# A Fourier mixing layer with a feed-forward layer behind it: input of the second in units of four columns s, other block sizes at both ends, and stages placed anew

## The chip, the core and the metric

The kernel runs on one NeuronCore of a Trainium2 chip. Its engines work side by side, each through its own list of instructions in order: TensorE (PE in the profile; PEld are its weight loads), VectorE (DVE), ScalarE (ACT), GpSimd (POOL) and SyncE (SP), of which the last two issue most transfers (DMAs) here. An instruction that has to wait for another engine holds up everything behind it in its own list. The metric is device time in microseconds (us), taken from the runs without the profiler; one more execution was recorded by the profiler, and all durations below come from it.

## The reference

```python
X = np.fft.rfft(x, axis=1)                  # x: 8 batches x 3008 tokens x 256 features
Y = X * (filt_r + 1j * filt_i)[None]
x = np.fft.irfft(Y, n=3008, axis=1).reshape(8 * 3008, 256)
h = x @ w_in                                # 256 x 2048
g = np.maximum(h, 0.0) + alpha * np.minimum(h, 0.0)
out = g @ w_out                             # 2048 x 256
```

The inputs and the output are float32. The kernel computes with float16 operands and float32 sums.

## The kernel before

**The two layers.** The Fourier layer is done as matmuls, with 3008 = 47 x 64: a token is 64 * s1 + s, with s1 from 0 to 46 and s from 0 to 63. Its result for two batches at a time lies in the SBUF tile yT, with the features on the partitions and 2 x 3008 columns, one for each token. The feed-forward layer reads columns of yT in blocks. A block of 512 columns (class Block) has 16 steps. Step j does `up(j)`: two matmuls that give 128 of the 2048 hidden features, into one half of a PSUM tile hps of two halves (two such tiles exist). After each second step ACT copies the pair from hps to SBUF as gtb (L420), and DVE applies the slope alpha in three instructions (two at L423, one at L424). In the same steps the block before does its `down(j)` (L433): in all, for each 128 columns, 16 matmuls that sum over the hidden features into a PSUM tile op, which ACT copies out as osb (L438); SP stores it to the output (L396). A block needs the last gtb of a pair of ups only in a late part of the next block's first steps: with n groups of 128 columns, step q of the next block does the downs n*q to n*q+n-1, and each 128 columns need all 16 hidden tiles.

There are four pairs of batches. `sizes` is the same for each: five blocks of 512 columns, one of 384, six of 512, so 12 blocks and 192 steps a pair, 768 steps in all.

**The Fourier stages.** They are cut into pieces that are put between the steps by hand: `put(step, ...)` notes a piece for a step, and it is issued just ahead of that step's ups. Each piece takes one of two PSUM banks (psF), which it holds until ACT or DVE has copied the result out; which of the two is decided when the program is built. The pieces of a batch are:
- a, 16 of them (L164): the first transform, copied by ACT (asb); after each four of them `save_a` writes to DRAM, and `turn_a` reads all back turned (at).
- b, 12 (L184): the second transform; DVE reads the result twice, for the products ww and uu (L188, L189). POOL moves ww across the partitions (sw), and from batch 2 on DVE adds both (`piece_s`).
- c, 12 (L209): the first inverse transform, copied by ACT (v); `turn_c` writes v to DRAM and, after the last, reads it back as zt.
- d, 16 (L231): the last transform, copied into yT by ACT.

`plan_fft(b, a0, ga, ta, b0, gap, add, lag, d0, ...)` gives a batch its steps: the a pieces from a0 every ga steps, `turn_a` at ta, the b pieces from b0 every gap steps, c lag steps behind b, d from d0. Batch 0 (class First) has no DRAM in between: its c pieces are followed by t pieces (L310, transposes on PE, copied to zt) and d pieces. Four t and four d of it stand ahead of the first block, the other twelve of each are put into the first 47 steps. `neg` (L476) makes the negated filter for batches 1 and on in steps 27 to 33.

**The order inside yT.** The columns of a batch are not in the order of tokens. Before, they lie in four groups of 752 columns (16 values of s), each with two halves of 376 for the two halves of s (0 to 31, 32 to 63), as wi3 gives both halves at once; inside, 47 values of s1 by eight values of s. A d piece gives four of the eight values of s for 128 of the 256 features, so its copy writes runs of four columns, and four d pieces fill 752 columns. The order that matters around the change is:

```python
g, dh, mh = i // 4, (i // 2) % 2, i % 2
t0 = self.base + g * 752
```

and a store of 128 columns (`store`) is cut where a run of 376 columns ends, since each run goes to its own rows of the output, eight rows in a run.

Of the kernel before, what the change touches and what calls it, by code (L numbers as in the profile page):

```python
# [13 lines left out]
NFFT = 3008  # L14
N1 = 47
N2 = 64
NK1 = 24
D = 256
NB = 8
DFF = 2048  # L20
NH = 32
# [43 lines left out]
def kernel(  # L65
# [53 lines left out]
    yT = konst.tile([128, 2, 2 * NFFT], FP16, name="yT")  # L119
# [5 lines left out]
    def load_x(b, c):  # L125
        xs = p_x.tile([2 * N1, 8 * D], FP16, name="xs")
        for h in range(2):
            nc.gpsimd.dma_start(out=xs[h * N1 : h * N1 + N1], in_=xrow(b, h, c))  # L128
        return xs
# [12 lines left out]
    def bank(wide=False):  # L142
        if wide:
            return psH.tile([128, 2, 512], FP32, name="hps")[:, 0]
        return psF.tile([128, 512], FP32, name="psF")


    class Fft:
# [75 lines left out]
                    nc.sync.dma_start(out=self.zt[:, s], in_=v_dram[self.b, :, s])  # L224

        def piece_d(self, i, evict, wide=False):
            g, dh, mh = i // 4, (i // 2) % 2, i % 2
            pd = bank(wide)
            ps = pd[:, 0 : 8 * N1].rearrange("p (m x) -> p m x", m=4)
            for m in range(4):  # L230
                nc.tensor.matmul(ps[:, m], self.zt[:, 8 * g + 4 * mh + m, dh * 128 : dh * 128 + 128],  # L231
                                 wi3_s, start=True, stop=True)
            t0 = self.base + g * 752
            evict(yT[:, dh, t0 : t0 + 752].rearrange("p (x m) -> p x m", m=8)[:, :, 4 * mh : 4 * mh + 4],
                  ps.rearrange("p m x -> p x m"))

    def on_act(o, i):
        nc.scalar.activation(o, i, AF.Copy)  # L238
# [4 lines left out]
    both = (on_act, on_dve)  # L243
# [72 lines left out]
    f0 = First()  # L316
# [24 lines left out]
    def warm(n):  # L341
        pw = psO.tile([128, 2, D], FP32, name="op")
        for _ in range(n):
            nc.tensor.matmul(pw[:, 0, 0:128], id16, id16, start=True, stop=True)
# [25 lines left out]
            f0.piece_b(kp + 2)  # L370
    nc.gpsimd.dma_start(out=filts_s[0:64], in_=filt_s[64:128])
    warm(8)
    for i in range(4):
        f0.piece_t(i, both[i % 2], i % 2 == 1)
    warm(4)
    for i in (0, 2, 1, 3):
        f0.piece_d(i, both[i // 2], i > 1)


    sizes = [512] * 5 + [384] + [512] * 6  # L380
    blocks = []
    for p in range(NB // 2):
        t = 0
        for n, tn in enumerate(sizes):
            blocks.append((p, t, tn, 2 * p + (n >= 6)))
            t += tn

    def store(p, t0, osb, lane):
        t = t0
        while t < t0 + 128:  # L390
            b, r = 2 * p + t // NFFT, t % NFFT
            blk, o = r // 376, r % 376
            n = min(t0 + 128 - t, 376 - o)
            g, h = blk // 2, blk % 2
            row = b * NFFT + (o // 8) * N2 + NH * h + 8 * g
            nc.sync.dma_start(  # L396
                out=bass.AP(tensor=out.tensor, offset=out.offset + row * D,
                            ap=[[N2 * D, n // 8], [D, 8], [1, D]]),
                in_=osb[t - t0 : t - t0 + n, lane])
            t += n  # L400

# [2 lines left out]
    class Block:  # L404
# [22 lines left out]
        def down(self, q):  # L427
            n = self.tn // 128
            for w in range(n * q, n * (q + 1)):
                si, k = w // 16, w % 16  # L430
                if si % 2 == 0 and k == 0:
                    self.op = psO.tile([128, 2, D], FP32, name="op")
                nc.tensor.matmul(self.op[:, si % 2], self.gts[k][:, 128 * si : 128 * si + 128],  # L433
                                 wout_s[:, k], start=(k == 0), stop=(k == 15))
                if k == 15 and (si % 2 == 1 or si == n - 1):
                    m = si % 2 + 1
                    osb = p_osb.tile([128, 2, D], FP32, name="osb")
                    nc.scalar.activation(osb[:, 0:m], self.op[:, 0:m], AF.Copy)  # L438
                    for lane in range(m):
                        store(self.p, self.t0 + 128 * (si - m + 1 + lane), osb, lane)  # L440
# [3 lines left out]
    def put(step, fn, *args):  # L444
        plan.setdefault(step, []).append((fn, args))

    def plan_fft(b, a0, ga, ta, b0, gap, add, lag, d0, quarters, x_at):
        f = Fft(b)
        for i in range(16):
            put(int(a0 + ga * i), f.piece_a, i, on_act)  # L450
        for c in range(4):
            put(int(a0 + ga * (4 * c + 3)), f.save_a, c)
            if b + 1 < NB:
                put(x_at[c],
                    lambda b=b, c=c: xc.update({(b + 1, c): load_x(b + 1, c)}))
        for q in range(quarters):
            w = NK1 // quarters
            put(ta, f.turn_a, nc.sync, w * q, w * q + w)
        bs = [b0 + (2 * int(gap * kp / 2) if add else int(gap * kp)) for kp in range(12)]
        for kp in range(12):  # L460
            put(bs[kp], f.piece_b, kp)
            if add:
                put(bs[kp] + add, f.piece_s, kp)
            put(bs[kp] + lag, f.piece_c, kp, on_act)
        for q in range(4):
            put(bs[3 * q + 2] + lag + 1, f.turn_c, q)
        for i in range(16):
            put(d0 + min(i, 4) + 2 * max(i - 4, 0), f.piece_d, i, on_act)

    for g, t0, d0, gap, evs in ((1, 0, 6, 1, both), (2, 17, 25, 2, (on_dve,)), (3, 32, 40, 2, (on_act,))):  # L470
        for i in range(4):
            put(t0 + gap * i, f0.piece_t, 4 * g + i, evs[i % len(evs)])
            put(d0 + gap * i, f0.piece_d, 4 * g + i, evs[i % len(evs)])

    def neg(ka, kb):
        nc.vector.tensor_scalar(filts_s[64:128, ka:kb], filt_s[64:128, ka:kb], -1.0, None, OP.mult)  # L476
# [1 line left out]
        nc.gpsimd.dma_start(out=filt_s[64:128, ka:kb], in_=filt_s[0:64, ka:kb])  # L478

    for i in range(4):  # L480
        put(27 + 2 * i, neg, 6 * i, 6 * i + 6)
    plan_fft(1, 16, 1, 32, 40, 2.75, 0, 7, 92, 4, (20, 24, 72, 73))
    plan_fft(2, 66, 2, 97, 109, 4.5, 8, 13, 187, 4, (110, 114, 118, 122))
    for b in range(3, NB):
        p = 96 * (b - 1)
        plan_fft(b, p - 68 - 2 * (b > 3), 2.4 + 0.1 * (b > 3), p - 27, p + 5, 5, 8, 13, p + 91, 1, (p + 6, p + 10, p + 16, p + 20))

    prev = None
    step = 0
    for p, t0, tn, _ in blocks:  # L490
        blk = Block(p, t0, tn)
        for j in range(16):
            for fn, args in plan.pop(step, ()):
                fn(*args)
            blk.up(j)
            if prev is not None:
                prev.down(j)
            step += 1
        prev = blk
# [33 lines left out]
```

## Time and profile before

| | |
|---|---|
| three runs without the profiler | 797.7, 797.81, 800.44 us |
| median | 797.81 us |
| the profiled execution | 799.4 us |
| its span, first to last instruction | 797.5 us |
| first matmul of the first block (L414) | 39.37 us |
| first down (L433) | 50.57 us |
| start of block 6 (step 96), after 2944 columns | 141.07 us |
| one block of 16 steps without pieces (steps 704 to 751) | 13.89 us |
| a block with a, b and c pieces (steps 208 to 255) | 16.67 to 17.05 us |
| L420, ACT, 128x1024 / 128x768 | 1022 / 809 ns, 352 / 32 times |
| L423, DVE, 128x512 / 128x384 | 354 / 316 ns, 704 / 64 times |
| L424, DVE, 128x1024 / 128x768 | 692 / 558 ns, 352 / 32 times |
| L438, ACT, 128x512 / 128x256 | 594 / 379 ns, 92 / 4 times |
| L188 and L189, DVE, each | 683 / 679 ns, 84 times each |
| L238, ACT, copies of a / c / d | 594 / 595 / 484 ns |
| L241, DVE, copies of t / d | 681 / 542 ns |
| SP's waits for ACT ahead of stores (L396) | 152.6 + 110.3 + 56.2 + 42.4 us |

The span is the time from the first to the last instruction of the profiled execution. What was timed without the profiler has a median 0.3 us above that span. A duration in the profile of a PE, DVE or ACT instruction can overlap with the next one's start on the same engine, so that the distance from start to start, in the timeline, is what one costs where the engine is full. PE matmuls, for one: those of 512 columns have a mean duration of 379 ns and start 0.216 us apart.

### The profile page before, as it was taken

What the parts mean: (1) busy time and instruction counts of PE and PEld (TensorE: products, weight loads), DVE (VectorE), ACT (ScalarE), POOL (GpSimd) and SP (SyncE); (2) the same over time, 40 slices, a digit from 0 to 9 for tenths busy, and PEclk for the clock granted to TensorE, in tenths of its full rate; (3) what the DMA queues carried; (4) which work ended last, traced back from release to release, by engine and by line L of the source; (5) the groups of instructions that cost most, each with busy time, mean ns of one, the idle gap of its engine ahead of it and who ended that gap; (6) DMA issues with size and microseconds to landing.
All of it is one profiled execution on the core that took longest, in us unless ns stands there. A gap on an engine that the chain in (4) does not pass through costs nothing.

```text
span 797.5 us, 16176 instructions
## 1 busy us (share of the span) xinstructions
PE 778.6 (98%) x5980; PEld 542.8 (68%) x5980; DVE 645.7 (81%) x1449; ACT 597.6 (75%) x836; POOL 141.5 (18%) x272
## 2 busy tenths in 40 slices
PE   6999999999999999999999999999999999999997
PEld 6756667666667666766667666766666766776665
DVE  4787996798879987798877988799877999777773
ACT  3678678877778887788768877788877867686663
POOL 7511330132103210132102321032100221000000
PEclk9999999999999999999999999999999999999999
DMA  9967448574655447474483545754484243511111
GB/s 179 211 143 181 132 106 223 157 169 115 150 153 121 110 125 173 126 142 129 119 207 83 119 127 141 177 112 113 123 179 117 54 106 85 138 38 28 41 40 53
DMA packets 94360, 100.59 MB, mean 126 GB/s; under 512 B 11369, under 2 KB 82041, under 8 KB 94217
## 3 DMA queue, kind: packets, MB, share of 16 engines
q1 hardware_dynamic: 79512, 68.80, 32.8%
q0 software_dynamic: 14768, 30.75, 19.7%
q8 instruction: 47, 0.77, 0.4%
q14 instruction: 33, 0.26, 0.1%
HBM read 56.26 MB, written 46.66 MB: 129 GB/s over the span
## 4 chain that ended last, share of the span: by engine, by line
PE 90%; ACT 3%; DMA 2%; DVE 1%; issue 1%; SPq 1%; POOL 0%; ACTq 0%; DVEq 0%; POOLq 0%
PE op L433 39%; PE hps L414 39%; PE psF L164 3%; PE psF L231 3%; PE psF L209 2%; PE psF L184 2%; ACT gtb L420 2%; DMA xs<-in_x_dram 1%; DMA filt_s<-in_filt_i_dram 1%; ACT osb L438 1%; PE hps L281 1%; DMA a_dram<-asb 1%; ACT v L238 1%; SPq L396 1%; PE psF L310 1%
## 5 line engine op out<-in xcount | busy, mean ns | idle before, releaser
L420 ACT ACTIVATE gtb<-hps 128x1024 f16<-128x1024 f32 (+1 forms) x384 | 385.4, 1004 | 126.5 <-PE hps L414 126.1
L433 PE MATMUL op<-wout_s,gtb 128*128 128x256 f16 x3008 | 451.1, 272 | 0.6 <-DVE gtb L424 0.6
L414 PE MATMUL hps<-yT,win_s 128*128 128x512 f16 (+1 forms) x1536 | 449.1, 374 | 0.4 <-ACT gtb L420 0.2
L433 PEld LDWEIGHTS <-gtb 128*128 128x128 f16 x3008 | 293.2, 97 | 189.6 <-DVE gtb L424 0.9
L423 DVE TENSOR_SCALAR m<-gtb,alm_s 128x512 f16<-128x512 f16 (+1 forms) x768 | 237.9, 351 | 99.5 <-ACT gtb L420 97.3
L424 DVE TENSOR_TENSOR gtb<-gtb,m 128x1024 f16<-128x1024 f16 (+1 forms) x384 | 261.5, 681 | 24.8 <-PE hps L414 0.9
L191 POOL DMA_DIRECT2D sw<-ww x168 | 87.8, 527 | 483.8 <-DVE ww L188 480.9
L414 PEld LDWEIGHTS <-win_s 128*128 128x128 f16 x1536 | 144.9, 98 | 32.3 <-issue 4.3
L238 ACT ACTIVATE asb<-psF 96x512 f16<-96x512 f32 x112 | 66.5, 594 | 16.4 <-PE psF L164 16.3
L238 ACT ACTIVATE yT<-psF 128x376 f16<-128x376 f32 x120 | 58.1, 484 | 22.9 <-PE psF L231 22.5
L438 ACT ACTIVATE osb<-op 128x512 f32<-128x512 f32 x96 | 56.2, 585 | 6.1 <-issue 3.2
L188 DVE TENSOR_TENSOR ww<-psF,filts_s 128x512 f16<-128x512 f32 x84 | 57.4, 683 | 0.0
L189 DVE TENSOR_TENSOR uu<-psF,filt_s 128x512 f16<-128x512 f32 x84 | 57.1, 679 | 0.0
L238 ACT ACTIVATE v<-psF 128x512 f16<-128x512 f32 x84 | 50.0, 595 | 4.3 <-PE psF L209 4.3
L164 PE MATMUL psF<-xs,wf_s 94*96 94x512 f16 x112 | 42.6, 381 | 2.5 <-ACT v L238 2.1
L231 PE MATMUL psF<-wi_s,zt 96*128 96x94 f16 x504 | 41.9, 204 | 0.9 <-ACT yT L238 0.7
L128 POOL DMA_DIRECT2D xs<-in_x_dram x64 | 34.0, 542 | 29.6 <-PE psF L164 14.8
L231 PEld LDWEIGHTS <-zt 96*128 96x128 f16 x512 | 35.5, 97 | 5.1 <-issue 1.5
L184 PE MATMUL psF<-at,twf_s 128*128 128x256 f16 x168 | 32.0, 272 | 2.7 <-ACT v L238 1.7
L209 PE MATMUL psF<-uu,twi_s 128*128 128x256 f16 x168 | 33.4, 273 | 0.0
L196 DVE TENSOR_TENSOR uu<-uu,sw 128x512 f16<-128x512 f16 x72 | 30.1, 418 | 0.0
L209 PEld LDWEIGHTS <-twi_s 128*128 128x128 f16 x192 | 18.6, 98 | 2.8 <-DVE uu L189 0.4
(57 smaller groups left out, 200.0 us busy)
## 6 DMA issues: line engine op xcount, KB each, us to landing
out_dram<-osb SPq DMA_DIRECT2D x128, 128.0 KB
xs<-in_x_dram POOLq DMA_DIRECT2D x64, 188.0 KB, 4.4
a_dram<-asb SPq DMA_DIRECT2D x28, 384.0 KB
sw<-ww POOLq DMA_DIRECT2D x168, 64.0 KB, 2.1
v_dram<-v SPq DMA_DIRECT2D x112, 96.0 KB
zt<-v_dram SPq DMA_DIRECT2D x28, 384.0 KB
at<-a_dram SPq DMA_DIRECT2D x20, 384.0 KB
at<-a_dram SPq DMA_DIRECT2D x32, 96.0 KB
```

Of the source, the lines that this page charges most:

```text
L164: nc.tensor.matmul(ps[0:96], wf1_s, xs[:, o : o + 512], start=True, stop=True)
L188: nc.vector.tensor_mul(ww, px, filts_s[:, 2 * kp : 2 * kp + 2])
L191: nc.gpsimd.dma_start(out=sw[o : o + 64], in_=ww[64 - o : 128 - o])
L209: nc.tensor.matmul(pv[:, kh], twi_s[:, k1], u[:, kh], start=u is us[0], stop=u is us[-1])
L231: nc.tensor.matmul(ps[:, m], self.zt[:, 8 * g + 4 * mh + m, dh * 128 : dh * 128 + 128], wi3_s, start=True, stop=True)
L238: nc.scalar.activation(o, i, AF.Copy)
L414: nc.tensor.matmul(self.hps[:, j % 2, 0:tn], win_s[:, kt, j * 128 : (j + 1) * 128], yT[:, kt, self.t0 : self.t0 + tn], start=(kt == 0), st ...
L420: nc.scalar.activation(g[:, :, 0:tn], self.hps[:, :, 0:tn], AF.Copy)
L423: nc.vector.tensor_scalar(m[:, i, 0:tn], g[:, i, 0:tn], 0.0, a, OP.min, OP.mult)
L424: nc.vector.tensor_add(g[:, :, 0:tn], g[:, :, 0:tn], m[:, :, 0:tn])
L433: nc.tensor.matmul(self.op[:, si % 2], self.gts[k][:, 128 * si : 128 * si + 128], wout_s[:, k], start=(k == 0), stop=(k == 15))
L438: nc.scalar.activation(osb[:, 0:m], self.op[:, 0:m], AF.Copy)
```

## The change

The columns of yT now lie in units of four s: 16 runs of 188 columns to a batch (47 values of s1 by four of s), two of them (376 columns, one for each half of s) for each two d pieces. The numbering of d pieces changes with it: pieces 0 and 1 are now the two halves of the features for the same four s, and together they fill the first 376 columns; a piece's copy writes its 376 columns without a gap. A store is cut at each 188 columns, with four rows in a run: 312 stores in the built kernel, 248 before.

In the first pair the blocks have 256, 384, four times 512, 256 and six times 512 columns, so 13 blocks; in the last, 384 and 128 stand in place of the last 512. There are 800 steps, and the first pair has 16 more, so everything of batch 2 and later moves by 16 steps.

Ahead of the first block there are now two t and two d pieces. The other fourteen of each lie in steps 0 to 47 (t) and 4 to 68 (d), and DVE copies the t pieces but one and eleven of the d pieces. Batch 1 has its a at 20 to 38, `turn_a` at 40, b from 46 every 3.25 steps, d from 107 (before: 16 to 31, 32, 40 and 2.75, 92). Batch 2 has its a from 64 every 2.5 steps, `turn_a` at 103, b from 121 every 5, d from 203 (before: 66 and 2, 97, 109 and 4.5, 187). From batch 3 on the a pieces come in fours at 0, 5, 7 and 8 of ten steps in place of every 2.4 or 2.5. `neg` begins at 31, not 27.

```diff
         def piece_d(self, i, evict, wide=False):
-            g, dh, mh = i // 4, (i // 2) % 2, i % 2
+            g, mh, dh = i // 4, (i // 2) % 2, i % 2
...
-            t0 = self.base + g * 752
-            evict(yT[:, dh, t0 : t0 + 752].rearrange("p (x m) -> p x m", m=8)[:, :, 4 * mh : 4 * mh + 4],
-                  ps.rearrange("p m x -> p x m"))
+            t0 = self.base + 376 * (i // 2)
+            evict(yT[:, dh, t0 : t0 + 376].rearrange("p (x m) -> p x m", m=4), ps.rearrange("p m x -> p x m"))
...
     warm(8)
-    for i in range(4):
-        f0.piece_t(i, both[i % 2], i % 2 == 1)
+    for i in range(2):
+        f0.piece_t(i, both[i], i == 1)
     warm(4)
-    for i in (0, 2, 1, 3):
-        f0.piece_d(i, both[i // 2], i > 1)
-
-
-    sizes = [512] * 5 + [384] + [512] * 6
+    for i in range(2):
+        f0.piece_d(i, both[i], i == 1)
+
+
+    sizes = [[512] * 5 + [384] + [512] * 6 for _ in range(NB // 2)]
+    sizes[0] = [256, 384] + [512] * 4 + [256] + [512] * 6
+    sizes[-1] = [512] * 5 + [384] + [512] * 5 + [384, 128]
...
-            blk, o = r // 376, r % 376
-            n = min(t0 + 128 - t, 376 - o)
-            g, h = blk // 2, blk % 2
-            row = b * NFFT + (o // 8) * N2 + NH * h + 8 * g
+            half, o = r // 188, r % 188
+            n = min(t0 + 128 - t, 188 - o)
+            row = b * NFFT + (o // 4) * N2 + NH * (half % 2) + 4 * (half // 2)
...
-                            ap=[[N2 * D, n // 8], [D, 8], [1, D]]),
+                            ap=[[N2 * D, n // 4], [D, 4], [1, D]]),
...
-    def plan_fft(b, a0, ga, ta, b0, gap, add, lag, d0, quarters, x_at):
+    def plan_fft(b, sa, ta, b0, gap, add, lag, d0, quarters, x_at):
...
-            put(int(a0 + ga * i), f.piece_a, i, on_act)
+            put(sa[i], f.piece_a, i, on_act)
...
-            put(int(a0 + ga * (4 * c + 3)), f.save_a, c)
+            put(sa[4 * c + 3], f.save_a, c)
...
-    for g, t0, d0, gap, evs in ((1, 0, 6, 1, both), (2, 17, 25, 2, (on_dve,)), (3, 32, 40, 2, (on_act,))):
-        for i in range(4):
-            put(t0 + gap * i, f0.piece_t, 4 * g + i, evs[i % len(evs)])
-            put(d0 + gap * i, f0.piece_d, 4 * g + i, evs[i % len(evs)])
+    for i, t in zip(range(2, 16), (0, 1, 15, 17, 19, 21, 33, 35, 37, 39, 41, 43, 45, 47)):
+        put(t, f0.piece_t, i, on_act if i == 2 else on_dve)
+    for i, t in zip(range(2, 16), (4, 5, 20, 23, 26, 27, 39, 41, 52, 54, 58, 60, 66, 68)):
+        put(t, f0.piece_d, i, on_act if i in (2, 4, 6) else on_dve)
...
-        put(27 + 2 * i, neg, 6 * i, 6 * i + 6)
-    plan_fft(1, 16, 1, 32, 40, 2.75, 0, 7, 92, 4, (20, 24, 72, 73))
-    plan_fft(2, 66, 2, 97, 109, 4.5, 8, 13, 187, 4, (110, 114, 118, 122))
+        put(31 + 2 * i, neg, 6 * i, 6 * i + 6)
+    plan_fft(1, [int(20 + 1.25 * i) for i in range(16)], 40, 46, 3.25, 0, 7, 107, 4, (26, 31, 73, 80))
+    plan_fft(2, [int(64 + 2.5 * i) for i in range(16)], 103, 121, 5, 8, 13, 203, 4, (122, 126, 132, 136))
     for b in range(3, NB):
-        p = 96 * (b - 1)
-        plan_fft(b, p - 68 - 2 * (b > 3), 2.4 + 0.1 * (b > 3), p - 27, p + 5, 5, 8, 13, p + 91, 1, (p + 6, p + 10, p + 16, p + 20))
+        p = 96 * (b - 1) + 16
+        sa = [(121 if b == 3 else p - 91) + 21 + 10 * (i // 4) + (0, 5, 7, 8)[i % 4] for i in range(16)]
+        plan_fft(b, sa, sa[15] + 5, p + 5, 5, 8, 13, p + 91, 1, (p + 6, p + 10, p + 16, p + 20))
```

Step numbers below count from the first block. A letter with a number, as d10, is the piece and its place in its batch, from 0.

More of the change, by code (lines that the diff above doesn't have):

```diff
@@ L383 @@
         t = 0
-        for n, tn in enumerate(sizes):
-            blocks.append((p, t, tn, 2 * p + (n >= 6)))
+        for tn in sizes[p]:
+            blocks.append((p, t, tn))
             t += tn
@@ L480 @@
     for i in range(4):
-        put(27 + 2 * i, neg, 6 * i, 6 * i + 6)
-    plan_fft(1, 16, 1, 32, 40, 2.75, 0, 7, 92, 4, (20, 24, 72, 73))
-    plan_fft(2, 66, 2, 97, 109, 4.5, 8, 13, 187, 4, (110, 114, 118, 122))
+        put(31 + 2 * i, neg, 6 * i, 6 * i + 6)
+    plan_fft(1, [int(20 + 1.25 * i) for i in range(16)], 40, 46, 3.25, 0, 7, 107, 4, (26, 31, 73, 80))
+    plan_fft(2, [int(64 + 2.5 * i) for i in range(16)], 103, 121, 5, 8, 13, 203, 4, (122, 126, 132, 136))
     for b in range(3, NB):
-        p = 96 * (b - 1)
-        plan_fft(b, p - 68 - 2 * (b > 3), 2.4 + 0.1 * (b > 3), p - 27, p + 5, 5, 8, 13, p + 91, 1, (p + 6, p + 10, p + 16, p + 20))
+        p = 96 * (b - 1) + 16
+        sa = [(121 if b == 3 else p - 91) + 21 + 10 * (i // 4) + (0, 5, 7, 8)[i % 4] for i in range(16)]
+        plan_fft(b, sa, sa[15] + 5, p + 5, 5, 8, 13, p + 91, 1, (p + 6, p + 10, p + 16, p + 20))
     prev = None
     step = 0
-    for p, t0, tn, _ in blocks:
+    for p, t0, tn in blocks:
         blk = Block(p, t0, tn)
```

## The prediction

> **What bounds the kernel now.** First the page: its busy shares (part 1) and the shares of the chain that ended last (part 4).
>
> ```profile
> PE 778.6 (98%) x5980; PEld 542.8 (68%) x5980; DVE 645.7 (81%) x1449; ACT 597.6 (75%) x836; POOL 141.5 (18%) x272
> ...
> PE 90%; ACT 3%; DMA 2%; DVE 1%; issue 1%; SPq 1%; POOL 0%; ACTq 0%; DVEq 0%; POOLq 0%
> ```
>
> TensorE sets the end, and the change removes no matmul of it. So I looked for the time in which PE did not issue. From the timeline's matmul starts: 512 columns take 0.216 us from start to start, 256 take 0.109, 94 take 0.041, a transposing matmul of L310 0.089. So a piece costs PE: a 0.22, t 4 x 0.089 = 0.36, d 4 x 0.041 = 0.165, b 0.22, c 0.22 (0.43 in batch 1, which has four). With these, all work from the first block's first up matmul (39.37) to the end is 740.9 us, so it could end at 780.3. It ends at 792.5: 12.2 us are lost. The starts of L414 put them by block of 16 steps: 5.6 in blocks 0 to 5 (39 to 141 us), 2.2 in blocks 8 and 9, 3.4 in the later batches, 0.8 at the end, 0.2 elsewhere.
>
> The timeline shows the kind of loss, at step 66:
>
> ```profile
> 106.83 0.38 PE L184 MATMUL psF<-at,twf_s 128*128 128x256 f16 x2
> ...
> 108.55 1.02 ACT L420 ACTIVATE gtb<-hps 128x1024 f16<-128x1024 f32 x1 [0.38 <-PE hps L414]
> ...
> 109.01 0.68 DVE L188 TENSOR_TENSOR ww<-psF,filts_s 128x512 f16<-128x512 f32 x1
> 109.11 0.27 PE L209 MATMUL psF<-sw,twi_s 128*128 128x256 f16 x1
> ...
> 109.47 0.59 ACT L238 ACTIVATE v<-psF 128x512 f16<-128x512 f32 x1
> 109.61 0.68 DVE L189 TENSOR_TENSOR uu<-psF,filt_s 128x512 f16<-128x512 f32 x1
> ...
> 110.11 0.38 PE L164 MATMUL psF<-xs,wf_s 94*96 94x512 f16 x1 [0.73 <-ACT v L238]
> ```
>
> The c piece ends at 109.4, ACT copies v out until 110.06, and the a piece of the same step, which has the same one of the two psF banks, stands until 110.11: 0.89 us more than back to back. The second thing to see: the b piece issued at 106.83 is read by DVE from 109.01 to 110.29. DVE is 3.4 us behind PE, and a bank filled for DVE is held that long.
>
> DVE's pace in the first block, where it is saturated:
>
> ```profile
> 48.42 0.61 DVE L423 TENSOR_SCALAR m<-gtb,alm_s 128x512 f16<-128x512 f16 x2
> ...
> 49.06 0.69 DVE L424 TENSOR_TENSOR gtb<-gtb,m 128x1024 f16<-128x1024 f16 x1
> ...
> 49.67 0.61 DVE L423 TENSOR_SCALAR m<-gtb,alm_s 128x512 f16<-128x512 f16 x2
> ```
>
> One pair of ups costs DVE 1.25 us here, not the 1.40 that durations add up to. The end:
>
> ```profile
> 786.87 5.63 PE L433 MATMUL op<-wout_s,gtb 128*128 128x256 f16 x50 [0.59 <-DVE gtb L424]
> 789.09 0.60 ACT L438 ACTIVATE osb<-op 128x512 f32<-128x512 f32 x1 [3.23 <-issue]
> 792.58 0.60 ACT L438 ACTIVATE osb<-op 128x512 f32<-128x512 f32 x1 [2.90 <-PE op L433]
> ```
>
> **The change, part by part**, against the span of 797.5.
>
> *Start.* The first up now needs two t and two d pieces, not four and four. t1 is copied by DVE by 37.8, d0 and d1 by 38.9, so it starts at about 38.9, not 39.37: -0.5. The other two of each, 2 x (0.36 + 0.165) = 1.05, now lie in the loop: net +0.6.
>
> *Ramp, blocks 0 to 6 (2944 columns, as blocks 0 to 5 before).* No row has a 256-column pair. By the step from 512 to 384 (L423 starts 0.269 and 0.235 apart, L424 0.61 and 0.475) it is 0.84 on DVE; ACT's 128x512 rows give 0.595 (interval 0.48). Bounds: half of 1.25, and 1.04, the 384 pair. The two small blocks in place of one cost DVE 3.4 us more, and 10 copies move from ACT to DVE (6 t x 0.60 + 4 d x 0.46 = 5.4). Load in blocks 0 to 4: PE 70.7, DVE 73.0, ACT 51.7; before, PE 81.6, DVE 72.6. So DVE, which had 9 us of slack, has none. I walked each queue in order by these intervals, with the banks that the built kernel gives its pieces:
> - Block 0: ACT and its hand-over, 0.64 a pair, against PE 0.43; from 38.7 to 44.5 against 4.9 of work: lost 0.9. DVE is at 48.3 when it ends its last pair.
> - Block 1 (0.54 us a step): t at step 19 needs t4's bank, which DVE frees at 47.5: 1.1. d at 20 waits for t5's copy: 0.5, and the a behind it for ACT: 0.75. Then a pieces in the one ACT bank at consecutive steps, where the copy's round is 1.1 to 1.5: 1.75. Together 4.1.
> - Block 2: 0.4.
> - Block 3: c at 53 stands in the bank of d at 52, which DVE reaches late: 1.85; c at 56 behind d at 54: 0.55; b at 59 behind c of that step: 0.9; two more, 0.7. Together 4.0.
> - Block 4: steps 66, 69 and 79 have c and then a in one bank: 3 x 0.89 = 2.7. c at 66 behind b at 65: 1.05; c at 69 behind d at 68: 1.35; one more 0.2. Together 5.3.
>
> Behind each wait stand all later ups and downs on PE, so each counts in full: 14.7. But each wait lets DVE catch up, so such a list overstates: before, c at 69 two steps behind b in its bank cost nothing. I take 13. Lowest: the four same-bank follows by ACT (3.6), block 0 (0.7) and an ACT-bound block 1 (1.5): 5.8. Highest: DVE 3.4 behind at each wait on it: +3.1, 17.8. Against 5.6 before, the ramp costs +7.4 (+0.2 to +12.2).
>
> By the granted clock this region ran at 1.00, though the stretch 10 to 20 us, with single gaps of 1.2, had 0.92. [...]
>
> *Batch 2 and later.* The a pieces of batch 3 on go to places (0, 5, 7, 8 of ten) where no c or b is, and batch 2's b get the later batches' gap of 5. Before, a behind c cost 1.11 (step 140), 0.56 (145) and 0.51 (153), and then 0.51 once in each of four batches, ACT having copied osb, v and asb in a row:
>
> ```profile
> 285.96 0.59 ACT L438 ACTIVATE osb<-op 128x512 f32<-128x512 f32 x1
> ...
> 287.09 0.38 PE L184 MATMUL psF<-at,twf_s 128*128 128x256 f16 x2 [0.35 <-ACT v L238]
> ```
>
> Now c follows b in its bank by three steps, 3.3 us; here DVE ends 2.5 after b's issue (182.50 to 185.03). So nothing waits: 1.11 + 0.56 + 4 x 0.51 + 0.51 = -4.2. It could be -2 if ACT still copies three in a row.
>
> *End.* Behind the last up stand 3 + 14 downs of 0.109 (1.85 us) that don't need it; its ACT (0.38) and DVE copies (0.8 at 128 columns by the same step, 1.04 at most) take 1.4 or less: the wait of 0.76 goes. The last copy is 128x256, 0.38 not 0.60, and one store is issued behind it, not two of 0.62: -0.84. Together -1.6. 16 more steps of small matmuls cost PE nothing: columns and 0.057 us weight loads stay under 0.44 a step.
>
> *Queues.* 64 more stores on SP, 0.7 us each (three in 2.22 at 108.19): 45 us. SP waits for ACT over 450 us, which hides them. The last save of batch 1's a now goes at step 38 with no store between it and the at reads: copy 1.2, landing 2.7 (the chain's a_dram step), four issues of 0.44, landing 2.7: 8.4 against 8 steps of about 1 us to b at 46. 0.4 at most, taken into the ramp; with a store in between 0.7 more. On POOL the x loads move 6 to 8 steps, ahead of use by 11 or more; neg on DVE moves by 4 steps, used 8 or more later; batch 1's d start 18 steps behind turn_c, not 14. Nothing.
>
> **Sum:** 797.5 + 0.6 + 7.4 - 4.2 - 1.6 = 799.7. The profiled execution took 799.4 with a span of 797.5; the median of the runs is 797.81, so 0.3 over that span: 800.0.
>
> **Rivals.**
> - *A, the ramp loses no more than before* (5.6): 800.0 - 7.4 = 792.6. For it: block 0 is short, downs start at 44.5, not 50.57, and ACT has 5.4 us less. Against it: the four same-bank follows alone are 3.6. Chance 0.15.
> - *B, DVE's lag decides, and it is slower.* From block 1 on DVE never idles and runs 3.4 us behind as at step 64, so each c and t that follows a DVE piece waits its full lag: 17.8, so 804.8; it decides from a ramp loss of about 14.8, 801.8. For it: DVE's 73.0 against PE's 70.7. Against: the waits hand DVE idle time. Chance 0.31.
> - *C, the new places of a do not do what they should*: the 4.2 stays: 804.2. For it: osb, v and asb still share ACT. Against: no two pieces share a step. Chance 0.07.
> - Forecast: a ramp loss of 7 to 14.8, so 794 to 801.8: 0.47.
>
> **Numbers.** A measurement here tells 0.5%, 4.0 us: 793.8 and 801.8. Faster: 0.12 of A. Slower: B and C, 0.38. Same: the forecast and 0.03 of A, 0.50. Range 793.5 to 804.5, which leaves out about half of A and the ends of B and C; the forecast's own is 794 to 801.8.
>
> **What would show it.** First up near 38.9 and the first down near 44.5; a c start at step 53, and 66 and 69, more than 1 us behind its step; block 7's first up near 151 to 153; no a start over 0.3 us late from step 112 on; the last wait of PE on gtb gone and the last store landing some 4.2 us behind the last matmul. If the first up of block 7 comes before 146, my ramp is wrong and A holds.

## Result and profile after

The changed kernel takes 823.87 us (median of 6 runs, 821.84 to 824.25), the kernel before, run beside it, 798.69 (6 runs, 797.7 to 800.61): 1.0308 times as long, 95% interval 1.0289 to 1.0327. The forecast was 800.0, and the range ended at 804.5. The profiled execution's span is 821.6, 24.1 longer than that of before. Of all executions behind the times below, one, of e12, ran at a granted clock of 0.72 and took 1451.9 us; its ratio leaves that one out.

The page of the changed kernel, busy shares and chain:

```profile
PE 783.8 (95%) x6044; PEld 547.5 (67%) x6044; DVE 657.6 (80%) x1507; ACT 597.7 (73%) x843; POOL 141.2 (17%) x272
...
PE 79%; DMA 8%; DVE 4%; ACT 3%; SPq 2%; issue 1%; POOL 0%; ACTq 0%; POOLq 0%
```

PE's share of the chain went from 90% to 79%, and DMA's from 2% to 8%: about 50 us of the chain more than before lie in transfers. The waits view says which pieces stood for them (lost us, times, longest):

```profile
PEld L231 <- DMA zt<-v_dram: 11.1, 5, 3.7
...
PE psF L231 <- DMA zt<-v_dram: 9.7, 5, 3.5
...
PE psF L209 <- DVE yT L240: 3.1, 3, 1.4
```

L231 is the d piece. The first d of batches 2 to 6 (steps 203, 299, 395, 491, 587) stood 3.6, 2.1, 1.2, 3.1 and 0.6 for zt; before, none did. Only the last row is of the kind that the prediction was about, c behind a d piece that DVE holds.

Loss by block was measured as for the prediction: the length of a block less its matmuls at their distances from start to start.

| us | predicted | measured |
|---|---|---|
| first up, and 1.05 of t and d now in the loop | +0.6 | -0.7 (first up 37.66) |
| blocks 0 to 6 against 0 to 5 before | +7.4 (13.0 against 5.6) | +13.6 (19.2 against 5.6) |
| blocks after these | -4.2 | +10.7 (16.4 against 5.7) |
| end | -1.6 | about +0.3 |
| sum | +2.2 | +23.9 |

The first row needs care. Seven profiles, that of before among them, have the old first blocks and first stages. In four of them the clock stayed at 1.00 from 10 us up to the first block, and the first up came at 37.5 to 37.7. The other three show the clock at 0.50 for one or three times 3.41 us between 13 and 23.4 us (before: 18.4 to 21.9), and there it came at 39.1 to 40.5. The changed kernel's profile has no such stretch, so the 1.7 is mostly how the execution fell.

SP's own timeline around the end of a batch's FFT, where the save and the reads of at are batch 4's and v and zt are batch 3's (issues; start, time over the group, count):

```profile
322.08 0.38 SPq L169 DMA_DIRECT2D a_dram<-asb  x1
327.48 2.25 SPq L176 DMA_DIRECT2D at<-a_dram  x4
329.83 3.46 SPq L396 DMA_DIRECT2D out_dram<-osb  x3
333.33 1.93 SPq L218 DMA_DIRECT2D v_dram<-v  x4
338.65 1.73 SPq L224 DMA_DIRECT2D zt<-v_dram  x4
```

The same place in the kernel before:

```profile
302.71 0.32 SPq L169 DMA_DIRECT2D a_dram<-asb  x1
304.11 2.24 SPq L396 DMA_DIRECT2D out_dram<-osb  x3
306.46 2.31 SPq L176 DMA_DIRECT2D at<-a_dram  x4
311.23 1.55 SPq L396 DMA_DIRECT2D out_dram<-osb  x2
312.88 2.03 SPq L218 DMA_DIRECT2D v_dram<-v  x4
318.15 1.73 SPq L224 DMA_DIRECT2D zt<-v_dram  x4
```

In the changed kernel SP issues the save of a at 322.08 and then stands until 327.48, because the reads of at wait for the save to land: 5.4. Before, the same two stood 3.75 apart, and SP issued three stores in between. Behind them three stores take 3.46 to issue (before, two took 1.55), the v writes come at 333.33, and the reads of zt wait until 338.65 for these, 5.3 as before. The first d was due at about 340.4 and started at 342.47. The batch's whole last turn hangs on how fast single DMAs land, with stores ahead of them and beside them.

In the ramp the waits that the prediction's walk priced one by one are there. PE's timeline in blocks 2 (the first line) and 4:

```profile
77.55 0.38 PE L184 MATMUL psF<-at,twf_s 128*128 128x256 f16 x2 [1.28 <-DMA at<-a_dram]
...
103.91 0.28 PE L209 MATMUL psF<-uu,twi_s 128*128 128x256 f16 x1 [0.93 <-DVE uu L189]
...
105.20 0.38 PE L164 MATMUL psF<-xs,wf_s 94*96 94x512 f16 x1 [0.69 <-ACT v L237]
...
109.83 0.27 PE L209 MATMUL psF<-uu,twi_s 128*128 128x256 f16 x1 [1.25 <-DVE yT L240]
...
111.11 0.38 PE L164 MATMUL psF<-xs,wf_s 94*96 94x512 f16 x1 [0.68 <-ACT v L237]
...
111.76 1.01 PE L433 MATMUL op<-wout_s,gtb 128*128 128x256 f16 x4
112.57 1.06 PE L414 MATMUL hps<-yT,win_s 128*128 128x512 f16 x2
...
125.19 0.28 PE L209 MATMUL psF<-sw,twi_s 128*128 128x256 f16 x1 [1.04 <-DMA sw<-ww]
```

Against back to back these cost 1.09 and 0.85 at step 66 (walked: 1.05 and 0.89), and 1.42 and 0.85 at step 69 (1.35 and 0.89). Three things the walk did not have: the b of step 46 stands 1.45 for at (the first line; 0.4 at most was granted), a c at step 79 stands 1.21 for sw (the last), and from 111.8 on the matmuls take twice as long. The windows view (PE busy, PEld, DVE, ACT, POOL, then the granted clock, DMA share, GB/s):

```profile
108.40:111.80 3.40, 1.46 (x10) 0.74 (x9) 2.54 (x5) 0.88 (x2) 1.03 (x2) 1.00 0.03 7
111.80:115.20 3.40, 3.40 (x14) 1.81 (x13) 1.31 (x3) 1.49 (x3) 0.00 (x0) 0.50 0.56 147
```

3.4 us with little work, then 3.4 us at clock 0.50, which costs some 1.7. The same stands behind two of the zt waits, at 343.9 and at 535.0.

### The profile page after: what moved, and what is told of

It reads as the page before. It is cut to its first block, busy times and chain, and to the rows that moved or that the text cites. A ratio compares the mean times of both kernels' runs of the same rounds, so it can differ in the third digit from the quotient of the medians.

```text
span 821.6 us, 16481 instructions
## 1 busy us (share of the span) xinstructions
PE 783.8 (95%) x6044; PEld 547.5 (67%) x6044; DVE 657.6 (80%) x1507; ACT 597.7 (73%) x843; POOL 141.2 (17%) x272
## 4 chain that ended last, share of the span: by engine, by line
PE 79%; DMA 8%; DVE 4%; ACT 3%; SPq 2%; issue 1%; POOL 0%; ACTq 0%; POOLq 0%
PE op L433 34%; PE hps L414 33%; PE psF L164 3%; PE psF L231 3%; PE psF L209 2%; DMA v_dram<-v 2%; DMA zt<-v_dram 2%; PE psF L184 2%; DMA at<-a_dram 2%; ACT gtb L420 2%; DVE m L423 1%; SPq L396 1%; DVE gtb L424 1%; DMA xs<-in_x_dram 1%; DMA sw<-ww 1%
## 5 line engine op out<-in xcount | busy, mean ns | idle before, releaser
L420 ACT ACTIVATE gtb<-hps 128x1024 f16<-128x1024 f32 (+3 forms) x400 | 388.2, 971 | 130.5 <-PE hps L414 128.1
L433 PE MATMUL op<-wout_s,gtb 128*128 128x256 f16 x3008 | 458.3, 274 | 0.0
L414 PE MATMUL hps<-yT,win_s 128*128 128x512 f16 (+3 forms) x1600 | 456.3, 367 | 0.5 <-ACT gtb L420 0.4
L423 DVE TENSOR_SCALAR m<-gtb,alm_s 128x512 f16<-128x512 f16 (+3 forms) x800 | 243.4, 346 | 116.0 <-ACT gtb L420 113.6
L424 DVE TENSOR_TENSOR gtb<-gtb,m 128x1024 f16<-128x1024 f16 (+3 forms) x400 | 264.1, 660 | 25.0 <-PE hps L414 0.5
L414 PEld LDWEIGHTS <-win_s 128*128 128x128 f16 x1600 | 151.7, 98 | 33.0 <-issue 5.7
L237 ACT ACTIVATE yT<-psF 128x376 f16<-128x376 f32 x116 | 56.1, 484 | 38.8 <-PE psF L231 38.4
L237 ACT ACTIVATE asb<-psF 96x512 f16<-96x512 f32 x112 | 66.5, 594 | 18.4 <-PE psF L164 18.4
L438 ACT ACTIVATE osb<-op 128x512 f32<-128x512 f32 (+1 forms) x97 | 56.2, 580 | 1.7 <-PE op L433 1.7
L231 PE MATMUL psF<-wi_s,zt 96*128 96x94 f16 x508 | 43.2, 207 | 10.6 <-DMA zt<-v_dram 9.7
L231 PEld LDWEIGHTS <-zt 96*128 96x128 f16 x512 | 36.1, 99 | 16.1 <-DMA zt<-v_dram 11.1
```

Of the source, the lines that this page charges most:

```text
L414: nc.tensor.matmul(self.hps[:, j % 2, 0:tn], win_s[:, kt, j * 128 : (j + 1) * 128], yT[:, kt, self.t0 : self.t0 + tn], start=(kt == 0), st ...
L420: nc.scalar.activation(g[:, :, 0:tn], self.hps[:, :, 0:tn], AF.Copy)
L423: nc.vector.tensor_scalar(m[:, i, 0:tn], g[:, i, 0:tn], 0.0, a, OP.min, OP.mult)
L424: nc.vector.tensor_add(g[:, :, 0:tn], g[:, :, 0:tn], m[:, :, 0:tn])
```

## The experiments

Twelve kernels were run, in three groups, each with the kernel before beside it (797.57, 798.44 and 798.32). Ratios are against that.

### One part at a time: order on SP, units, places

**e1**, the changed kernel with the v writes and the zt reads on POOL's queue:

```diff
-                    nc.sync.dma_start(out=v_dram[...], in_=self.v[...])
+                    nc.gpsimd.dma_start(out=v_dram[...], in_=self.v[...])
...
-                    nc.sync.dma_start(out=self.zt[:, s], in_=v_dram[self.b, :, s])
+                    nc.gpsimd.dma_start(out=self.zt[:, s], in_=v_dram[self.b, :, s])
```

> The changed kernel, with the writes of v and the reads of zt (turn_c) issued on POOL's queue, not SP's. Theory 1 (the first d of batches 2 to 6 wait 10.5 us in all because v's writes and zt's reads stand in SP's queue behind the at reads, which wait for the last save of a to land, and behind stores): the zt waits at steps 203, 299, 395, 491, 587 go, and with them the two stretches at half clock behind them, so about 808 to 811. Rival 2 (the transfers themselves land late, whatever queue they are in): over 819. The ramp's 19 us of loss up to step 96 stay in both.

**e2**, the changed kernel with `turn_a` of batches 3 to 7 behind the previous batch's `turn_c`:

```diff
-        plan_fft(b, sa, sa[15] + 5, p + 5, 5, ...)
+        plan_fft(b, sa, p - 21 + 4 * (b == 3), p + 5, 5, ...)
```

> The changed kernel, with turn_a of batches 3 to 7 six steps later (ten for batch 3's last a to its turn_a), behind the last turn_c of the batch before. Theory 1: v's writes no longer stand behind the at reads, so the zt waits go: 808 to 811. Rival 3 (it is the 64 more stores that hold SP up, not the at reads): v's writes still come late behind stores, two thirds of the waits stay: 816 to 822.

**e3**, the kernel before with units of four s alone: the new numbering of d, runs of 188 columns, 312 stores; blocks and stages as before.

> The kernel before with the columns in units of four s alone (the new numbering of d, the new runs of 188 columns and with them 312 stores), old blocks and old steps. Theory 1: SP has slack of some microseconds ahead of each first d as long as the last save stands six steps ahead of turn_a: 798 to 801. Rival 3 (the stores): zt waits at the first d of batches 2 to 6, 805 to 812.

**e4**, the kernel before with the new places of a alone:

```diff
+        sa = [p - 70 + 4 * (b == 3) + 10 * (i // 4) + (0, 5, 7, 8)[i % 4] for i in range(16)]
```

> The kernel before with the new places of the a pieces of batches 3 to 7 alone (0, 5, 7, 8 of ten steps, the last save five steps ahead of turn_a, not six). What the prediction says of these places: the stalls of an a behind a c go, 4 x 0.51 us and up to 2 in blocks 8 and 9, and nothing comes for it: 795 to 797. Theory 1 with the save as its cause: the at reads wait for the later save and v's writes behind them: 803 to 812, with waits for zt at steps 283, 379, 475, 571.

Measured: e1 813.36 (1.0195, 1.0180 to 1.0210); e2 809.73 (1.0150, 1.0132 to 1.0168); e3 806.31 (1.0114, 1.0092 to 1.0136); e4 796.85 (0.9986, 0.9974 to 0.9998).

e1 lies 2.4 above its range and e2 inside it; e3 came out where its rival, the stores, had it, and e4 inside its range. e1 and e2 show the zt waits for what they are: with v and zt off SP's queue two are left (2.06 and 1.08), with at behind them none, and 10.5 and 14 us go. That says which queue, but not why SP's old order, in which at also went ahead of v, had done without a wait. e4 shows the new places as predicted: from block 12 on the longest blocks go from 17.05 to 16.74, and no a stands behind c there. Beside batch 2's b and c, which still come every 4.5 steps in e4, one a and one b still wait 0.4 each, so not all of the 4.2 was to be had. It gains 1.1, since a zt wait of 2.38 comes up at step 187. e3 is the one that speaks against the prediction: the units alone, with nothing moved, cost 1.1%. Its b at step 109 waited 3.4 for at:

```profile
PE psF L184 <- DMA at<-a_dram: 3.4, 1, 3.4
```

It had a zt wait of 1.25 too, and its last matmul was 8.0 ahead of the end, against 5.3 before. Each is a transfer that landed late. The only transfers that e3 changes are the stores.

### What is wrong with the stores

The DMA view of the changed kernel from 789 to 799 us, where few transfers but stores are under way, in 40 slices of 0.25 us, and one of the issues in it:

```profile
GB/s 66 0 0 0 115 12 4 0 0 119 217 57 16 16 25 33 45 53 33 29 29 33 25 25 25 25 20 25 25 25 21 193 311 21 70 29 0 0 160 217
...
out_dram<-osb SPq DMA_DIRECT2D x1, 92.0 KB
```

The store of 92 KB is issued at 790.73. From 792 to 796.5 the slices show 16 to 53 GB/s, most of them 25 or a little more, where slices with other stores reach 200 to 300. In the packet records these are single 1 KB packets, one after the other, 46 ns long and starting 42 ns apart, which is 24 GB/s. From 794.2 to 796.5, with little else under way, the DMA share is 0.07, about one of the sixteen DMA engines. 92 KB are 92 rows in 23 runs of four, and 23 has no divisor but itself and one.

From 725 us on, where the stores are nearly alone, most of them stand apart in the packet records. One of 29 runs takes 5.62 us from its first packet to the end of its last (116 packets) and one of 31 takes 5.91 (124), with at most 2 packets under way at once. One of 18 takes 0.58 (72 packets), and those of 22, 24, 26, 28 and 32 runs 0.60, 0.61, 0.62, 0.65 and 0.52, with 12 to 21 under way at once (this number is called the spread below). Seven groups of stores there have one of 17, 19, 23, 29 or 31 runs, and each has stretches of 0.7 us or more of single packets; the other seven groups have none over 0.3. Before, a store had at most 16 runs of eight rows. In that trace, from 700 us on, those of 8, 9, 11, 13 and 16 runs take at most 0.58, 0.59, 0.59, 0.62 and 0.73 us, with at most 11, 12, 15, 15 and 21 packets under way. With runs of four rows there are up to 32: 40 of the 312 stores have 17, 19, 23, 29 or 31, of 68 to 124 KB, by estimate 3 to 5 us each at 42 ns a packet. No run shows on how many engines a store goes, since the traces name none; where an expectation below counts them, what the traces show is the packets under way.

Rival: not the spread, but the number of stores on SP's queue.

**e5** is e3, and **e6** the changed kernel, with these stores cut at 16 runs, and those of 21, 22, 25 and 26 runs as well, 72 in all (one of 25, issued at 707.28, took 1.12 us with at most 8 packets under way; those of 22 and 26, at 0.60 and 0.62, were no slower than others):

```diff
             n = min(t0 + 128 - t, 188 - o)
+            if n // 4 in (17, 19, 21, 22, 23, 25, 26, 29, 31):
+                n = 64
```

> The kernel before with units of four s alone, but a store of 17, 19, 21, 22, 23, 25, 26, 29 or 31 runs is cut into 16 runs and the rest: 384 stores in place of 312 with uncut units, 248 before. [...] Cut, no store has fewer than 7 engines unless it is short: the wait of b at step 109 for at (3.58), that of d at 187 for zt (1.25) and the longer tail (2.7) go, 797 to 800. Rival (the count of stores on SP's queue is what costs): 72 more stores make it slower than units alone, 808 or more against its 806.3.

> The changed kernel with the same cut of its stores. Theory: the zt waits at the first d of batches 2 to 6 (10.5 in all, with two stretches at half clock of 1.7 each) shrink to 3 or less, the last store lands some 5.0 behind the last matmul, not 6.3: 808 to 813 against 823.9, with the ramp's loss of some 19 still there. Rival (count on SP): 72 more stores make it slower, 826 or more.

**e7** is the kernel before with 64 of its largest stores cut in two, so that it has the 312 stores of the changed kernel:

```diff
             n = min(t0 + 128 - t, 376 - o)
+            if t % 256 == 0 and n == 128:
+                n = 64
```

> The kernel before with 64 of its stores of 128 rows cut in two: 312 stores, as many as the changed kernel, each on 8 or 16 engines unless it is short. Theory: SP's waits hide them: 797 to 799.5. Rival (the count): 804 or more, as the units alone gave 806.3.

Measured: e5 800.58 (1.0026, 1.0014 to 1.0038) with 384 stores, where e3 had 1.0114 with 312. e6 811.81 (1.0177, 1.0148 to 1.0206) with 384, where the changed kernel had 1.0308 with 312. e7 798.99 (1.0015, 1.0005 to 1.0025) with 312. More stores made both kernels faster, and as many stores as the changed kernel's, well spread, cost 0.15%. The rival falls: it is the spread. (e5 ends 0.6 above its range, e6 and e7 inside theirs.) In e5 the wait for at is down from 3.4 to 0.9:

```profile
PE psF L184 <- DMA at<-a_dram: 0.9, 1, 0.9
```

At batch 4's turn the reads of at go 3.05 behind the save in e6, in place of 5.4. SP's issues shrink too: seven stores of the changed kernel took 2.1 to 5.7 us to issue, and none took over 1.8 in the kernel before or in e6. Whether at and zt come late by these issues or by the slow transfers beside them, the runs do not part.

The slow stretch is gone from e6's DMA view at the same stage of its end (783 to 793 us):

```profile
GB/s 0 0 61 70 0 0 156 197 98 201 4 16 98 0 0 131 17 0 0 0 0 0 0 0 0 0 0 0 0 0 279 246 0 98 0 25 225 12 0 143
```

And the end follows the last matmul by 4.9, where the changed kernel took 6.3. Of its five zt waits two are left, 3.24 at step 203 and 2.68 at 491: more than the 3 in all that was expected. The profiled execution of e6 took 815.63, 3.8 above the median, so these waits need not be typical. They point to the order on SP, taken up in e9.

### The ramp

**e8** is e6 with batch 2's a pieces moved off the steps that have a c:

```diff
-    plan_fft(2, [int(64 + 2.5 * i) for i in range(16)], 103, ...)
+    plan_fft(2, (64, 67, 70, 73, 76, 80, 83, 86, 89, 91, 93, 95, 96, 98, 99, 101), 103, ...)
```

> The changed kernel with the cut stores, and batch 2's a pieces of steps 66, 69, 71, 79 and some others moved to steps without a c piece. Theory of the ramp: each a behind c in the one bank of ACT costs 0.85, and three of them with the c waits at 66 and 69 bring the half clock at 112 to 115 (about 2): block 4's loss falls from 7.8 to 3.5, so 4 to 4.5 less than the changed kernel with cut stores alone. Rival (DVE's lag decides the ramp: 73.0 of work against PE's 70.7 in blocks 0 to 4): the waits move to other pieces, 1.5 less at most.

Measured: 810.37 (1.0142, 1.0124 to 1.0161), 1.4 less than e6. That is the rival's figure, and the two intervals overlap, so the time decides nothing. The traces do: e6's three waits of 0.85 of an a behind c are gone in e8, and what grew beside them are two waits for transfers, one for at by 0.4 (block 2) and one for sw of 0.86 (block 5). Block 4's loss went from 4.9 to 2.5. (The whole ramp's went from 17.4 to 14.8, but about 1.1 of that is a half clock in block 1 that e8's execution did not have, at the same steps.) So the same-bank follows are worth what the walk gave them (three of 0.85), but the expectation counted a half clock that e6 did not have at that place. There it was at 47.9 to 51.4, behind block 1's waits, and at 112 to 115 the clock stayed at 1.00 behind the same 1.42 and 0.85. More on that below.

**e9** is e8 with `turn_a` where e2 has it; **e10** is e9 with d pieces 10 to 15 copied by ACT:

```diff
-        put(t, f0.piece_d, i, on_act if i in (2, 4, 6) else on_dve)
+        put(t, f0.piece_d, i, on_act if i in (2, 4, 6) or i > 9 else on_dve)
```

> The changed kernel with cut stores, batch 2's a pieces off the c steps, and turn_a of batches 3 to 7 put behind the previous batch's turn_c on SP. Theory: what is left of the zt waits (9.6 in blocks 12 and 30, with the half clock that they bring) came of the reads of at and of the save they wait for, ahead of v and zt on SP; they go: 802.5 (800.5 to 804), all of what is lost against the kernel before now in the ramp. Rival (zt is late for another reason, such as the stores still on SP): 806 or more.

> As the one before, with the copies of the first batch's d pieces 10 to 15 (steps 52 to 68) on ACT, not DVE. Theory: c at 53, 56 and 69 stood behind d pieces that DVE reached late, 1.8 + 0.6 + 1.5; ACT, with 8 us to spare in blocks 3 and 4, copies them at once: 3 to 4 less. Rival (ACT gets in the way of c, a and g): 1 less at most.

Measured: e9 803.75 (1.0072, 1.0059 to 1.0086), e10 798.50 (1.0003, 0.9991 to 1.0015). In e9 no d waits for zt. SP's timeline there, at batch 5's turn:

```profile
507.96 1.88 SPq L218 DMA_DIRECT2D v_dram<-v  x4
511.45 1.77 SPq L224 DMA_DIRECT2D zt<-v_dram  x4
513.27 6.62 SPq L176 DMA_DIRECT2D at<-a_dram  x4
519.98 10.17 SPq L398 DMA_DIRECT2D out_dram<-osb  x11
```

The reads of zt go 3.5 behind the v writes, and those of at, which nothing needs soon, behind them. e10 gives 5.2, more than the 3 to 4 expected; the ramp's loss falls from 15.1 to 11.0. The waits of c for a d piece that DVE holds, in e9:

```profile
PE psF L209 <- DVE yT L240: 3.5, 3, 1.7
```

In e10 there is no such row. The windows of the changed kernel and of e10 from the end of block 2 into block 4:

```profile
76.00:98.00 22.00, 18.15 (x142) 12.58 (x140) 19.55 (x41) 11.13 (x14) 5.19 (x10) 1.00 0.52 141
98.00:116.00 18.00, 14.25 (x91) 8.97 (x90) 11.49 (x25) 9.33 (x14) 3.11 (x6) 0.91 0.22 60
```

```profile
76.00:98.00 22.00, 21.47 (x166) 15.05 (x165) 20.72 (x45) 14.25 (x21) 5.18 (x10) 1.00 0.48 132
98.00:116.00 18.00, 16.86 (x125) 11.68 (x124) 14.47 (x30) 13.77 (x21) 6.27 (x12) 1.00 0.45 107
```

ACT (the fourth busy figure) had 11 of 22 and 9 of 18 us to do; it takes on the copies without holding anything up, and PE is busy 21.5 of 22 us, not 18.2. DVE did not have too much work in all in this stretch (the third busy figure, 19.6 of 22 and 11.5 of 18 us in the changed kernel). It came too late to single pieces, and a bank that it held stopped PE. The two kernels differ by the cut stores, the moved a pieces and the order on SP as well; the price of the copies alone is e10 against e9.

### All but the first blocks, and a version that beats both

**e11** is the kernel before with the new places of a, `turn_a` behind the previous `turn_c`, and last blocks of 384 and 128; units of eight, first blocks and first stages are as before. **e12** is e11 with the units of four and the cut stores.

```diff
+    sizes[-1] = [512] * 5 + [384] + [512] * 5 + [384, 128]
...
+        sa = [p - 70 + 4 * (b == 3) + 10 * (i // 4) + (0, 5, 7, 8)[i % 4] for i in range(16)]
+        plan_fft(b, sa, p - 21 + (b == 3), p + 5, 5, ...)
```

> The kernel before, its units, first blocks and first stages as they were, with the new places of a for batches 3 to 7, turn_a behind the previous batch's turn_c, and last blocks of 384 and 128. The new places alone gave 796.85 with a wait for zt of 2.38 at step 187; that goes, and the end is 1.6 shorter: 792.9 (791.5 to 794.5), faster than both. If the wait stays: 795.3; if the end gives nothing: 794.5.

> As the one before with units of four s and cut stores: all of the change, mended, but the small first blocks and the stages that go with them. Theory: the units with cut stores cost 2 (as alone), so 795 (793.5 to 797), and the small first blocks with their stages cost what the mended changed kernel lies above it, 7 or so. Rival (the units are what is lost in the ramp too): 800 or more.

Measured: e11 793.82 (0.9947, 0.9934 to 0.9959), faster than both kernels; e12 796.66 (0.9981, 0.9972 to 0.9991). e11's span is 791.1 against e4's 795.0, with first ups at 37.58 and 37.53: 2.4 of the 3.9 is the zt wait, and the other 1.5 is the end. Both lie inside their ranges. The units, even well spread, cost 2.8 (e12 against e11; where, was not taken apart), and the small first blocks with their stages, mended as far as e9, 7.1 more, as e10 still 1.8.

## Why the prediction was wrong, point by point

- *Queues: the step that failed.* "64 more stores on SP [...] 45 us. SP waits for ACT over 450 us, which hides them [...] Nothing." The issue of 64 more stores is indeed hidden where they are well spread: e7 issues its 312 in 209 us in place of 170, and that costs 0.4 to 2.0. But the step priced the issue of a store alone, not its transfer. The packets of a store of 17, 19, 23, 29 or 31 runs go out one at a time (5.62 us for 29 runs, 0.65 for 28), the issues take 253 us, and the transfers of a, at, v and zt land late beside it. What the sum had at nothing is 13.9 at the first d pieces (10.5 of waits for zt and two half clocks of 1.7), and 1.0 more than granted for at. Cutting the stores brings 12.1 by the medians and 10.5 by the ratios (1.0308 to 1.0177), and no rival had that mechanism. The order on SP alone (e2) brings 14.1. The two overlap: with both, and e8's 1.4, e9 is 20.1 below the changed kernel, not 27.6. The diff shows what was missed, the new number of runs, `n // 4`.
- *Batch 2 and later, -4.2: right in mechanism, wrong in sum.* The a-behind-c stalls went; e2, without zt waits, loses 2.9 in these blocks against 5.7 before, so -2.8 where -4.2 was said. In block 8 about 0.65 of it is a c that waits for DVE to read the b ahead of it in its bank, three steps on: DVE is done 3.55 after that b's issue there, where the prediction took 2.5. What came in its place is the turn of a batch: the walk checked b's wait for at only for batch 1 and d's wait for zt nowhere but for batch 1. With b at every 5 steps, batch 2's `turn_c` goes 14 steps ahead of its first d, 16 before. e9 against e8 shows the order on SP alone to be worth 6.6 with cut stores, and e4 shows that the new places alone bring a zt wait even with the old stores.
- *Ramp, +7.4: right in mechanism, too small.* The walked list was 14.7 and was cut to 13, because waits let DVE catch up. They did not: the waits that were walked one by one came out within 0.3. The lumps did not (block 1's row of a pieces 1.3 for 1.75, block 2 1.4 for 0.4), but these two partly cancel, so the sum fits the list better than its parts do, which is luck. 19.2 less the wait for at (1.45), that for sw (1.21) and the half clock (1.7) is 14.8. The at wait was held to be "0.4 at most" from landings of 2.7; with cut stores (e6) it is 0.47.
- *Clock*: the sum has no price for it, and the ramp before ran at 1.00. In the changed kernel, waits of 1.42 and 0.85 were followed by 3.41 us at 0.50, which cost some 1.7.
- *End, -1.6: right for the last blocks, wrong here.* e11 shows 1.5. In the changed kernel the wait on gtb is gone too, but the last store lands 6.3, not 4.2, behind the last matmul, for the stores ahead of it are still trickling out; before it was 5.3.
- *Start, +0.6*: not to be told from this pair, since the 39.37 of before holds a half clock. Among the profiles without one ahead of the first block, the small first blocks begin at 36.6 to 37.7 and the old ones at 37.5 to 37.7.
- *Rivals.* B (DVE's lag, 17.8 in the ramp) had the ramp nearest, but by luck: 4.4 of the 19.2 are the at, the sw and the clock, which it did not have, and no c or t waited the full lag of 3.4 (longest 1.6). e10 bears out a part of it, that pieces held by DVE cost time. Its 804.8 is 19 short, since the ramp is 13.6 of the 24.1 at most. C falls: the new places do what they should. A falls: no kernel with the small first blocks lost less than 11.0 in the ramp.

## What to carry to other kernels

When a change alters the shape of a store or load, see in a trace how long the packets of each size that occurs take: here 124 KB in 31 runs took 5.91 us, and 128 KB in 32 took 0.52. A count of packets or of issues doesn't show it (e5 has 72 stores more than e3 and is 5.7 us faster), and a number of runs that goes badly can be cut into a round one and a rest, here 16 and what is left. A transfer that is off the critical path can still set when the transfers beside it land (e3's wait for at was 3.4, e5's 0.9), so price the longest chain of dependent DMAs (save, reads of at; v, reads of zt) with that traffic, for each batch and not for the first alone. On one in-order queue put what is needed next ahead of what waits for a landing. And where a piece stands because a loaded engine comes late to its bank, give that copy to an engine with time to spare, even if the loaded one isn't saturated over the stage.

## What the hardware showed that was not expected

*The stretches at half clock lie on a grid of 3.413 us.* In the changed kernel the stretches at 0.50 begin at 111.8, 343.9 and 535.0 us and last 3.41 each; the second and third begin 68.0 and 124.0 times 3.413 behind the first. In e6 they begin at 47.9, 242.5 (this one lasts twice 3.41) and 529.2, the later two 57.0 and 141.0 times 3.413 behind the first. Worked out from the matmuls' starts and columns, in the changed kernel PE had 2.27, 2.02 and 3.08 us without work in the 3.41 ahead of the three; no other window of this grid has more than 1.88 from 40 us to the last block, and in the kernel before, where no stretch at 0.50 lies between them, none has more than 1.16. So several short waits within a window went ahead of a stretch, not only a single long one: the first of the three has those of 1.42 and 0.85. These cost another 1.7 in the changed kernel and nothing in e6. That it depends on where the grid lies is the author's reading; no run moved the grid alone.

*A store whose packets go out one at a time moves 1 KB rows at some 24 GB/s* (42 ns from packet to packet), and one of 92 KB takes over 4 us. Whether all such stores share one engine was not shown, since the trace names none.
